# A gated attention and MLP mix on one core: TensorE and VectorE orders fixed by hand, LN1's apply moved to GpSimd, and four smaller moves

## The chip, the cores and the metric

One core of one Trainium2 chip. The metric is device time in microseconds of one execution; a quoted time is the median of the fast runs. "Span" is the length of one profiled execution, about 2 us shorter than its time. The mean granted TensorE clock of each profiled run is given where it matters.

The engines by their names in the profile: PE is TensorE (matmul), DVE is VectorE, ACT is ScalarE, POOL is GpSimd, SP is the sync engine, which here only issues DMA.

## The reference

Input x is 2048 rows of 640 bf16 values; 32 heads of 20.

```python
def _A_ref(x, wqkv, wo):                       # linear attention
    q, k, v = ...                              # x @ wqkv
    pq, pk = phi(q), phi(k)                    # phi(t) = where(t>0, t+1, exp(t)) + 1e-6
    kv  = einsum("bhsd,bhse->bhde", pk, v)
    z   = einsum("bhsd->bhd", pk)
    num = einsum("bhqd,bhde->bhqe", pq, kv)
    den = einsum("bhqd,bhd->bhq", pq, z)[..., None] + 1e-6
    return (num / den) @ wo                    # heads put together again

def _B_ref(x, w1, w2, w3, w4):
    h  = gelu(layernorm(x) @ w1)               # LN1, W1
    hs = concat(four column groups of h, shifted by 1, -1, 2, -2 rows) @ w2
    x1 = x + hs
    return x1 + gelu(layernorm(x1) @ w3) @ w4  # LN2, W3, W4

g = sigmoid((x * gate_w).sum(-1))
return g * A + (1 - g) * B
```

## The kernel before

The 2048 rows are 16 chunks of 128 rows, and 4 tiles of 4 chunks. `pair()` gives one of four PSUM buffers; whatever TensorE writes next needs one that its reader has given back. A framework orders the instructions of each engine and inserts all waits. The stages on TensorE, in order: wk (k for 16 chunks), q, g (x transposed times phi(k)), z, W1 of tile 0, kv, W1 of tile 1, W2 of tile 0, W1 of tile 2, den, W1 of tile 3, then for each tile a W3 and a W4 stage (the first W3 stage also holds the rest of W2, the m products and, before the change, the scaling of phi(q) by 1/den).

The profile's names: pp is a PSUM buffer (PSUM is the memory that TensorE writes to), pk is phi(k), pqT phi(q) transposed, zz the sum z in two bf16 parts, zT its transpose, zbd what den is multiplied with; omg is 1 - g, ehT a transpose on the way to it; r_bf holds ey / den, kvT the masked kv, lnxT a tile of LN1 transposed, hsT the GELU outputs at their shifted places. A "round trip" is VectorE writing a tile, a DMA transposing it, and VectorE reading it again.

Parts:

```python
    def gate_unit():                     # its first part (gate logits, exp into ey) is cut
        ...
        eh = area2.tile([P, 2, TS], BF16, tag="z")
        nc.vector.tensor_copy(eh[:, 0], ey[:])
        nc.vector.tensor_tensor(eh[:, 1], ey[:], eh[:, 0], op=ALU.subtract)
        ehT = area2.tile([P, 2 * CPT, P], BF16, tag="zT")
        nc.sync.dma_start_transpose(ehT[:], eh[:].rearrange("p k s -> p (k s)"))   # round trip 1
        nc.vector.tensor_tensor(omg[:]..., eT[...], eT[...], op=ALU.add)           # omg = 1 - g
        ...
    def z_unit():
        ...                                                                        # matmuls, then
        nc.vector.tensor_copy(zv[:, 0], pt[:, :, 0:HD])
        nc.vector.tensor_tensor(zv[:, 1], pt[:, :, 0:HD], zv[:, 0], op=ALU.subtract)
        nc.sync.dma_start_transpose(zT[:], zz[:])                                  # round trip 2
        nc.vector.tensor_reduce(zc[:], zT[:]..., op=ALU.add)
        ...                                                                        # zbd from zc
    def den_unit():                      # matmuls with zbd and pqT, then
        nc.vector.tensor_scalar_add(pt[:, 0, :], pt[:, 0, :], 1e-6)
        nc.vector.reciprocal(pt[:, 1, :], pt[:, 0, :])
        nc.vector.tensor_tensor(r_bf[:], pt[:, 1, :], ey[:], op=ALU.mult)

    def ln1_tile(t):
        lnxT[t] = lnx_p.tile([P, DC, TS], BF16, name="lnxT")
        for c in range(t * CPT, (t + 1) * CPT):
            ln_stats(mv1[:, c, :], x_sb[:, c, :], st1s[:, c])                      # DVE
        tt = slice(t * CPT, (t + 1) * CPT)
        rsqrt(rstd1[:, tt], mv1[:, tt, 1])                                         # GpSimd
        for c in range(t * CPT, (t + 1) * CPT):
            lnx = work.tile([P, D], BF16, name="ln")                               # 3 buffers
            nc.vector.tensor_scalar(lnx[:], x_sb[:, c, :], mv1[:, c, 0:1], rstd1[:, c:c + 1],
                                    op0=ALU.subtract, op1=ALU.mult)                # "the apply"
            cc = c % CPT
            nc.sync.dma_start_transpose(lnxT[t][:, :, cc * P:(cc + 1) * P], lnx[:])

    def w1_unit(t, fcs):
        ...                                                                        # matmuls on lnxT[t]
            if fc < 4:
                nc.scalar.activation(hsT[:, fc, o:o + TS], pt[:, i, :], ACT.Gelu_apprx_tanh)
            else:                                                                  # the fifth block
                for g in range(4):
                    nc.scalar.activation(hsT[32 * g:32 * (g + 1), 4, o:o + TS],
                                         pt[32 * g:32 * (g + 1), i, :], ACT.Gelu_apprx_tanh)
    ...
    for c in range(NCH):
        k_unit(c)
    for t in range(NT):
        for js in q_split:
            q_unit(t, js)
        if t == 1:
            gate_unit()
    ...
    for fc in range(DC):
        g_unit(fc)
    z_unit()
    ln1_tile(0)
    ln1_tile(1)
    ...                                  # W1 of tile 0, kv, W1 of tile 1, ln1_tile(2), ln1_tile(3)
```

## Time and profile before

| before | value |
|---|---|
| time, median of the first 3 runs | 287.79 us (287.67 to 288.4) |
| profiled span, mean clock | 286.1 us, 0.98 |
| PE busy, POOL busy | 273.3 us, 24.1 us |
| W1 of tile 1 starts | 87.95 us |
| first W3 stage | 114.5 to 143.2 us |

The page of the kernel before, the span in 40 slices of 7.15 us; each digit is tenths of a slice (9 is 90% or more), and PEclk is the granted clock in tenths:

```profile
PE   6999999999967999999899999999999999999994
...
POOL 8500100011213010000001000001000010000000
PEclk9999999999985999999999999999999999999999
```

TensorE is full but for the ends of the span, slices 12 and 13 and a small dip in slice 20, and its clock drops in slices 12 and 13. GpSimd is nearly idle. The waits of TensorE in the kernel before (what it waited for, microseconds in total, times, longest):

```profile
PE pp L285 <- DVE zz L261: 2.3, 1, 2.3
PE pp L358 <- DVE kvT L293: 2.2, 1, 2.2
...
```

Two waits of some weight after the head, one stage: the kv stage (L285) waited for the buffer that VectorE's zz gave back, and W1 of tile 1 (L358) for the one that kvT gave back. The timeline of TensorE in the kernel before (start, length, what, and in brackets the idle time ahead of it):

```profile
75.18 4.49 PE L358 MATMUL pp<-lnxT,w_sb 128*128 128x512 bf16 x20
79.51 1.24 PE L361 MATMUL pp<-lnxT,w1x 128*128 128x512 bf16 x5
83.06 2.65 PE L285 MATMUL pp<-wkq 128*120 128x120 bf16 x30 [2.31 <-DVE zz L261]
87.95 7.33 PE L358 MATMUL pp<-lnxT,w_sb 128*128 128x512 bf16 x20 [2.24 <-DVE kvT L293]
```

The same 20 W1 matmuls took 4.49 us for tile 0 and 7.33 us for tile 1: the clock records show 0.5 from 83.5 to 93.7 us. The Trainium skill says that an idle window takes the array to half its clock and a busy one back ("TensorE: Matmul & The Clock Gate", "What's actually happening"); this trace agrees as to the two states, and shows a drop after only 2.3 us of idle time. So a short wait costs more than its length.

### The profile page before, as it was taken

The numbers are of one execution on the slowest core, as the hardware profiler recorded it, in microseconds if no ns is written. First come the engines' busy times: TensorE is split into PE (matmuls) and PEld (weight loads), VectorE is DVE, ScalarE is ACT, GpSimd is POOL, SyncE is SP. The second block draws the span as 40 slices with busy tenths as digits, with TensorE's granted clock in tenths as the row PEclk, the third lists the DMA queues.
The fourth block names the chain that finished last, engine by engine and source line by source line (L and its number), as shares of the span: only waits on it lengthen the run. The fifth ranks groups of instructions, "written<-read, shape, count | busy, mean of one in ns | idle before, by whom it ended". The sixth has DMA issues, their size and how long they took to land.

```text
span 286.1 us, 4181 instructions
## 1 busy us (share of the span) xinstructions
PE 273.3 (96%) x1730; PEld 162.2 (57%) x1730; DVE 132.6 (46%) x266; ACT 92.0 (32%) x117; POOL 24.1 (8%) x47
## 2 busy tenths in 40 slices
PE   6999999999967999999899999999999999999994
PEld 3677444677542543544377655577655577545772
DVE  1588788888733367485625244034252045100121
ACT  1455435311440529732314022404033304143000
POOL 8500100011213010000001000001000010000000
PEclk9999999999985999999999999999999999999999
DMA  8999884025548804000002400003300007100001
GB/s 207 214 318 363 221 269 136 3 40 98 109 79 231 170 0 92 2 0 0 0 2 66 98 23 0 2 23 69 92 2 0 2 23 112 51 0 0 25 32 37
DMA packets 43464, 22.96 MB, mean 80 GB/s; under 512 B 33670, under 2 KB 42375, under 8 KB 43447
## 3 DMA queue, kind: packets, MB, share of 16 engines
q1 hardware_dynamic: 41669, 19.68, 28.1%
q0 software_dynamic: 464, 2.21, 2.3%
q10 hardware_dynamic: 1314, 0.82, 0.9%
q8 instruction: 13, 0.21, 0.3%
q14 instruction: 4, 0.03, 0.0%
HBM read 11.96 MB, written 2.62 MB: 51 GB/s over the span
## 4 chain that ended last, share of the span: by engine, by line
PE 78%; DVE 8%; DMA 6%; ACT 3%; issue 2%; POOL 1%; DVEq 0%; SPq 0%; ACTq 0%; POOLq 0%
PE pp L450 21%; PE pp L463 21%; PE pp L202 8%; PE pp L460 8%; PE pp L212 7%; PE pp L419 6%; DMA lnxT<-ln 4%; PE pp L358 3%; DMA x_sb<-in_A_x_dram 1%; DMA zT<-zz 1%; DVE st1s L185 1%; DVE ln L347 1%; POOL rstd_191 L182 1%; PE pp L303 1%; ACT ln L437 1%
## 5 line engine op out<-in xcount | busy, mean ns | idle before, releaser
L450 PE MATMUL pp<-lnxT,w_sb 128*128 128x512 bf16 x280 | 63.4, 379 | 1.2 <-ACT h_1268 L452 0.8
L450 PEld LDWEIGHTS <-w_sb 128*128 128x128 bf16 x280 | 27.1, 98 | 32.3 <-issue 2.5
L192 ACT ACTIVATE e<-pp 128x640 bf16<-128x640 f32 (+2 forms) x28 | 21.8, 780 | 24.0 <-PE pp L202 14.8
L460 PE MATMUL pp<-m_sb,pqT 128*128 128x320 bf16 x160 | 27.0, 299 | 0.0
L419 PE MATMUL pp<-w_sb,hsT 128*128 128x320 bf16 x160 | 23.9, 299 | 0.0
L202 PE MATMUL pp<-wkq,xT 128*128 128x320 bf16 x160 | 23.1, 308 | 0.0
L358 PE MATMUL pp<-lnxT,w_sb 128*128 128x512 bf16 x80 | 20.8, 422 | 2.2 <-DVE kvT L293 2.2
L212 PE MATMUL pp<-xT,wkq 128*128 128x512 bf16 x100 | 22.1, 379 | 0.0
L273 PE MATMUL pp<-pk,x_sb 128*128 128x320 bf16 x160 | 21.9, 299 | 0.0
L419 PEld LDWEIGHTS <-hsT 128*128 128x128 bf16 x160 | 15.4, 98 | 8.1 <-issue 0.7
L202 PEld LDWEIGHTS <-xT 128*128 128x128 bf16 x160 | 16.1, 101 | 6.7
L460 PEld LDWEIGHTS <-pqT 128*128 128x128 bf16 x160 | 15.7, 98 | 6.7
L273 PEld LDWEIGHTS <-x_sb 128*128 128x128 bf16 x160 | 15.7, 98 | 6.2
L463 PE MATMUL pp<-w_sb,h_1682 128*128 128x320 bf16 x112 | 16.5, 299 | 0.0
L463 PE MATMUL pp<-w_sb,h_2026 128*128 128x320 bf16 x112 | 16.5, 299 | 0.0
L463 PE MATMUL pp<-w_sb,h_2370 128*128 128x320 bf16 x112 | 16.5, 299 | 0.0
L463 PE MATMUL pp<-w_sb,h_1268 128*128 128x320 bf16 x112 | 16.5, 299 | 0.0
L212 PEld LDWEIGHTS <-wkq 128*128 128x128 bf16 x100 | 9.6, 98 | 11.6 <-issue 0.4
L358 PEld LDWEIGHTS <-w_sb 128*128 128x128 bf16 x80 | 8.3, 107 | 13.8 <-issue 4.5
L326 DVE TENSOR_TENSOR pqT<-pqT,pp 128x1024 bf16<-128x1024 bf16 x10 | 12.1, 1217 | 6.4 <-PE pp L323 6.3
L366 ACT ACTIVATE hsT<-pp 128x512 bf16<-128x512 f32 x16 | 8.6, 596 | 18.8 <-PE pp L358 18.8
L194 DVE SCALAR_TENSOR_TENSOR pk<-pp,e 128x640 bf16<-128x640 f32 x16 | 13.2, 825 | 1.7
(197 smaller groups left out, 280.7 us busy)
## 6 DMA issues: line engine op xcount, KB each, us to landing
out_dram<-oc SPq DMA_DIRECT2D x15, 160.0 KB, 2.0
w_sb<-in_B_w_dram SPq DMA_DIRECT2D x1, 2160.0 KB
w_sb<-in_B_w_dram POOLq DMA_DIRECT2D x1, 2080.0 KB, 11.0
x_sb<-in_A_x_dram SPq DMA_DIRECT2D x3, 640.0 KB, 8.5
wkq<-in_A_wqkv_dram SPq DMA_DIRECT2D x2, 800.0 KB, 9.8
wkq<-in_A_wqkv_dram ACTq DMA_DIRECT2D x2, 400.0 KB, 4.8
w_sb<-in_B_w_dram SPq DMA_DIRECT2D x1, 800.0 KB
wo_sb<-in_A_wo_dram SPq DMA_DIRECT2D x5, 150.0 KB, 9.3
```

What stands on the lines that cost most here:

```text
L192: nc.scalar.activation(ev, src, ACT.Exp)
L194: nc.vector.scalar_tensor_tensor(dst, src, 0.0, ev, op0=ALU.max, op1=ALU.add)
L202: nc.tensor.matmul(pt[:, hf, 0:c1 - c0], lhsT=xT[:, dc, cs], rhs=wk_sb[:, dc, c0:c1], start=(dc == 0), stop=(dc == DC - 1))
L212: nc.tensor.matmul(pt[:, i, :], lhsT=wq_sb[:, dc, j * P:(j + 1) * P], rhs=xT[:, dc, ts_], start=(dc == 0), stop=(dc == DC - 1))
L273: nc.tensor.matmul(pt[:, hf, 0:HD], lhsT=x_sb[:, c, fc * P:(fc + 1) * P], rhs=pk[:, c, hf * HD:(hf + 1) * HD], start=(c == 0), stop=(c == ...
L326: nc.vector.tensor_tensor(sl, sl, pt[:], op=ALU.mult)
L358: nc.tensor.matmul(pt[:, i, :], lhsT=w1_sb[:, dc, CG * fc:CG * fc + P], rhs=lnxT[t][:, dc, :], start=(dc == 0), stop=(dc == DC - 1))
L366: nc.scalar.activation(hsT[:, fc, o:o + TS], pt[:, i, :], ACT.Gelu_apprx_tanh)
L419: nc.tensor.matmul(pt[:, hf, 0:HD], lhsT=hsT[:, fc, 2 + c * P:2 + (c + 1) * P], rhs=w2_sb[:, fc, hf * HD:(hf + 1) * HD], start=(fc == 0), ...
L450: nc.tensor.matmul(pt[:, i, :], lhsT=w3_sb[:, dc, fc * P:(fc + 1) * P], rhs=lnT[:, dc, :], start=(dc == 0), stop=(dc == DC - 1))
L460: nc.tensor.matmul(pt[:, hf, 0:HD], lhsT=pqT[:, j, c * P:(c + 1) * P], rhs=m_sb[:, j, hf * HD:(hf + 1) * HD], start=(j == 0), stop=False)
L463: nc.tensor.matmul(pt[:, hf, 0:HD], lhsT=h2[:, fc, cc * P:(cc + 1) * P], rhs=w4_sb[:, fc, hf * HD:(hf + 1) * HD], start=False, stop=(fc == ...
```

## The change

Its intent: keep the two stalls around kv from arising, by fixing TensorE's and VectorE's orders by hand, by taking LN1's apply off VectorE, by moving the den product ahead of W1 of tile 0, and by moving the scaling out of the crowded first W3 stage into W1. Also a new head (four chunks transposed on TensorE, wk by halves), the fifth block's GELU in one piece with GpSimd copying it to its shifted places, and LN2 chunk by chunk. Cut to its core:

```diff
     def ln1_tile(t):
 ...
-            nc.vector.tensor_scalar(lnx[:], x_sb[:, c, :], mv1[:, c, 0:1], rstd1[:, c:c + 1],
+            nc.gpsimd.tensor_scalar(lnx[:], x_sb[:, c, :], mv1[:, c, 0:1], rstd1[:, c:c + 1],
                                     op0=ALU.subtract, op1=ALU.mult)
 ...
+                hx = hxp.tile([P, TS], BF16, name="hx")
+                nc.scalar.activation(hx[:], pt[:, i, :], ACT.Gelu_apprx_tanh)
                 for g in range(4):
-                    nc.scalar.activation(hsT[32 * g:32 * (g + 1), 4, o:o + TS], pt[32 * g:32 * (g + 1), i, :], ...)
+                    nc.gpsimd.tensor_copy(hsT[32 * g:32 * (g + 1), 4, o:o + TS], hx[32 * g:32 * (g + 1), :])
 ...
+    pe_dve = {mybir.EngineType.PE, mybir.EngineType.DVE}
+    with tc.manual_schedule(engines=pe_dve):
+        ...                                  # head: four chunks transposed on TensorE, wk by halves
+        g_unit(0)
+        ln1_tile(0)
+        g_unit(1)
+        omg_unit()                           # was part of gate_unit, in the q stage
+        z_unit()                             # was after the five g blocks
+        ln1_tile(1)
+        g_unit(2)
+        ln1_tile(2)
+        g_unit(3)
+        ln1_tile(3)
+        g_unit(4)
+        den_unit()                           # was after W1 of tile 2
+        for fcs in w1_split:
+            w1_unit(0, fcs)
+        for gs in ((0, 1), (2, 3), (4, 5)):
+            kv_unit(gs)
+        for i, fcs in enumerate(w1_split):
+            w1_unit(1, fcs)
+            scale_unit(i)                    # the scalings were in the first W3 stage
 ...
+        nb = small.tile([P, 1], F32, name="nb2")            # LN2, for each chunk
+        nc.gpsimd.tensor_scalar(nb[:], mv[:, 0:1], rstd[:], -1.0, op0=ALU.mult, op1=ALU.mult)
 ...
+    with tc.manual_schedule(engines={mybir.EngineType.PE}):
+        ...                                  # W2, W1 of tiles 2 and 3 with 7 scalings, W3 and W4
```

GpSimd, ScalarE and the sync engine keep the orders that the framework finds.

## The prediction

> **What bounds the kernel now.** TensorE: busy 273 of the 286.1 us span (busy shares), 78% of the chain that ended last. From 143 to 282 us its matmuls run back to back (timeline: 0.216 us per 512-column matmul, 0.136 per 320): nothing to win there. What it loses lies earlier:
>
> - Head: warm-up, two transposed chunks, first wk matmul at 6.05 us, nine of them at half clock (0.267 us each) until 8.4 us.
> - The kv stage (80.8 to 96.3 us): 2.3 us idle until VectorE's zz gave back a PSUM pair, kv at half clock (2.65 us), 2.2 us idle until the kvT copies, which sat in VectorE's order behind the 3.5 us zz transpose, then W1 of tile 1 in 8.4 us instead of 5.4. The granted clock is 0.5 from 83.5 to 93.7 us. Together some 8.4 us, the only large loss. The Trainium skill ("TensorE: Matmul & The Clock Gate", "What's actually happening") says an idle window throttles the array; this trace agrees, after only 2.3 us idle.
> - W1 of tile 3 and first W3 stage: 0.5 + 0.5 + 0.8 us of waits for ScalarE.
>
> **What the change does, costed.**
> 1. Head: two more chunks transposed on TensorE (0.53 us each at half clock). The half-wk order hides a DMA wait the trace does not have: the half clock, not wk, made the first unit slow. I expect 0 to 0.6 us lost.
> 2. LN1's apply (16 x 0.36 us) and its waits for the rsqrt leave VectorE. But VectorE's order is now fixed, with two DMA round trips inside: omg and z (3.5 us each). Summed with trace durations from its last phi (55.5): statistics of tile 0 4.2, omg 1.1 + 3.5 + 0.6, zz 1.7, transpose 3.5, zbd 1.3, twelve chunk statistics at 1.04 = 12.5, den 4.8 (the reciprocal 3.36): about 88.5 to 89.5 us.
> 3. TensorE: g, z, den done at 77, W1 tile 0 at 82.3, kv (1.6 at full clock) at 84. Then den's pair and kv's three, all four PSUM pairs, wait for VectorE. W1 tile 1 cannot start before about 89: roughly 5 us idle, then half clock for some 5 us (2 to 3 us lost). The old stall in two pieces returns as one of about the same cost, 7 to 8 us. This is the step that decides.
> 4. Scaling: 10 x 0.32 us of TensorE work stay, only elsewhere. The first W3 stage falls from 28.8 to about 24.3 us, W1 tiles 1 to 3 grow by 3.2. Saved: waits there, about 1.3 us, plus 0.6 in W1 of tile 3, as GELU's four 32-partition pieces (2.4 us ScalarE) become one of 0.6 plus GpSimd copies (estimate 0.6 each from its 0.71 us select of 32x640).
> 5. GpSimd: 16 applies, estimated 0.7 to 1.2 us each from its memset rate (0.9 ns per element); hidden.
>
> Sum: 75.7 + den 1.2 + W1 5.4 + kv 1.6 + stall 5.4 + W1 8.2 + W2 5.4 + W1 10.8 + scaling 3.2 + W3 24.3 + unchanged rest 142.9 = 284.1 us span, time 1.7 more: **285.6 us**, 8 in 10 between 281.5 and 289.5. Faster by over 2%: 0.19; within: 0.77; slower: 0.04.
>
> **What would show it.** Right: TensorE idle near 84 to 89 us, released by VectorE's den or kvT; clock 0.5 after it; no wait at scaling; W3 first stage near 24 us; the rest unchanged. Wrong: no gap over 2 us after kv.
>
> **What would make it wrong.** VectorE reaching den before 84 us removes stall and half clock: about 278 us. The omg or z transpose queued behind LN1's on the DMA queue, or kv's first pair taking den's slot: 287 to 289.

## More of the kernel before

VectorE's group for the apply, and the sync engine's queue, in the kernel before:

```profile
L347 DVE TENSOR_SCALAR ln<-x_sb,mv_190,rstd_191 128x640 bf16<-128x640 bf16 x16 | 6.5, 443 | 5.9 <-POOL rstd_191 L182 4.8 <-DMA lnxT<-ln 1.0
```

```profile
61.26 18.20 SPq L350 DMA_TRANSPOSE lnxT<-ln  x12
82.94 1.33 SPq L262 DMA_TRANSPOSE zT<-zz  x1
```

Sixteen applies are 6.5 us of VectorE in all, 443 ns each (neighbouring records overlap a little). All DMA transposes go through one queue, in one order: z's comes after twelve of LN1's, but those are done by 79.5 us, and it does not wait for them.

## The result, and the profile after

| | before | after |
|---|---|---|
| time, median of 4 runs | 288.1 us (287.67 to 289.18) | 314.55 us (314.14 to 314.86) |
| ratio, 95% interval | 1 | 1.0911 [1.0876, 1.0946] |
| profiled span, clock | 286.1 us, 0.98 | 312.4 us, 0.943 |
| PE busy | 273.3 us | 276.9 us |
| POOL busy | 24.1 us | 85.7 us |

The change is slower by 9.1%, far outside the predicted range. The slices of the kernel after (7.81 us each):

```profile
PE   5999999998480915969999999999999999999995
...
POOL 8301000292089999636120100210102101000000
PEclk9899999999596675899999999999999999999999
```

The hole in TensorE's row is now slices 10 to 18, GpSimd is full in slices 13 to 16, and the clock is low in most of slices 11 to 17. The waits of TensorE, after:

```profile
PE pp L445 <- POOL hsT L377: 10.3, 2, 10.2
PE pp L363 <- DMA lnxT<-ln: 8.6, 1, 8.6
PE pp L323 <- DVE zbd L276: 5.2, 1, 5.2
...
PE pp L363 <- DVE pqT L337: 1.8, 1, 1.8
```

W2 waited 10.2 us for GpSimd's copies, W1 of tile 1 waited 8.6 us for a transposed LN1 tile, den waited 5.2 us for VectorE's zbd. The same stretch of TensorE's timeline, after:

```profile
82.08 2.32 PE L323 MATMUL pp<-pqT,zbd 128*32 128x512 bf16 x20 [5.25 <-DVE zbd L276]
...
90.47 1.76 PE L295 MATMUL pp<-wkq 128*120 128x120 bf16 x30
100.88 0.59 PE L363 MATMUL pp<-lnxT,w_sb 128*128 128x512 bf16 x1 [8.64 <-DMA lnxT<-ln]
...
121.00 7.09 PE L445 MATMUL pp<-w_sb,hsT 128*128 128x320 bf16 x30 [10.15 <-POOL hsT L377]
...
138.86 2.32 PE L363 MATMUL pp<-lnxT,w_sb 128*128 128x512 bf16 x10 [1.81 <-DVE pqT L337]
```

The kv stage itself (L295) now runs at full clock in 1.76 us instead of 2.65, so the half clock of that stage is repaired. What comes before and after it is lost. Thirty W2 matmuls took 7.09 us, where 30 x 0.136 = 4.1 us is full clock. Now who is late? The group of the apply, GpSimd's timeline, and ScalarE's line for the GELU that the copies read, after:

```profile
L352 POOL TENSOR_SCALAR ln<-x_sb,mv_174,rstd_175 128x640 bf16<-128x640 bf16 x16 | 39.9, 2501 | 0.5
```

```profile
62.61 9.97 POOL L352 TENSOR_SCALAR ln<-x_sb,mv_174,rstd_175 128x640 bf16<-128x640 bf16 x4
86.67 0.23 POOL L170 TENSOR_SCALAR rstd_175<-mv_174 128x4 f32<-128x4 f32 x1 [14.09 <-DVE mv_174 L177]
...
88.15 9.96 POOL L352 TENSOR_SCALAR ln<-x_sb,mv_174,rstd_175 128x640 bf16<-128x640 bf16 x4
...
110.95 7.48 POOL L352 TENSOR_SCALAR ln<-x_sb,mv_174,rstd_175 128x640 bf16<-128x640 bf16 x3
118.38 2.56 POOL L377 COPY hsT<-hx 32x512 bf16<-32x512 bf16 x4
```

```profile
90.67 0.60 ACT L374 ACTIVATE hx<-pp 128x512 bf16<-128x512 f32 x1
```

The apply takes 2501 ns on GpSimd; it took 443 ns on VectorE. A tile of four is 10 us. The copies show a second harm: those that W2 of tile 0 needs could have run from 91.3 us, when hx was there, but in GpSimd's order they stand behind the applies of tile 1, of tile 2 and three of tile 3, and came at 118.38 us, though W1 of tile 1 was done at about 110. And between tiles 0 and 1 GpSimd stood idle for 14.09 us, waiting for VectorE's statistics (mv). Why were those late? The sync engine's queue, after:

```profile
65.16 6.17 SPq L355 DMA_TRANSPOSE lnxT<-ln  x3
71.42 2.39 SPq L247 DMA_TRANSPOSE ehT<-eh  x1
73.90 1.25 SPq L355 DMA_TRANSPOSE lnxT<-ln  x1
78.10 1.33 SPq L272 DMA_TRANSPOSE zT<-zz  x1
```

and the one line of VectorE's timeline, after, that waits for it:

```profile
75.85 0.18 DVE L249 TENSOR_TENSOR omg<-ehT 128x16 f32<-128x16 bf16 x1 [14.27 <-DMA ehT<-eh]
```

VectorE had eh ready at 61.6 us. Its transpose stood in the queue behind three LN1 transposes, which came as GpSimd made them, 2.5 us apart. VectorE, whose order is now fixed, waited 14.27 us, and zz, zbd and the statistics of tiles 1 to 3 waited behind it. VectorE's chain (statistics 82.5 to 94.4, den 94.5 to 99.2, kvT to 100.6) and GpSimd's (tile 1 applied at 98.1, its last transpose landed by 100.9) then released W1 of tile 1 at nearly the same time. So at this last step either alone would have kept it until about 100.6 us. They are not two independent causes, though: GpSimd's tile 1 was late because it had waited 14.09 us for VectorE's statistics, and those stood behind VectorE's wait for ehT, which had stood behind GpSimd's tile 0.

The shift, stage by stage, read from the timelines:

| event on TensorE | before | after | shift | grown by |
|---|---|---|---|---|
| wk stage ends | 28.9 | 30.7 | +1.8 | +1.8 |
| g and z end | 75.2 | 76.8 | +1.6 | -0.2 |
| W1 of tile 1 starts | 87.95 | 100.88 | +12.9 | +11.3 |
| W2 of tile 0 starts | 96.2 | 110.1 | +13.9 | +1.0 |
| first W3 stage starts | 114.5 | 145.5 | +31.0 | +17.1 |
| first W3 stage ends | 143.2 | 169.6 | +26.4 | -4.6 |
| end | 286.1 | 312.4 | +26.3 | -0.1 |

Two stretches lose 28 us, the first W3 stage wins 4.6 us (the scalings, 3.2 us, and 1.25 us of waits for ScalarE are gone), and nothing after it moved.

### The profile page after: what moved, and what is told of

It is laid out like the page before. It is cut to its first block, busy times and chain, and to the rows that moved or that the text cites. A ratio compares the mean times of both kernels' runs of the same rounds, so it can differ in the third digit from the quotient of the medians.

```text
span 312.4 us, 4265 instructions
## 1 busy us (share of the span) xinstructions
PE 276.9 (89%) x1726; PEld 163.4 (52%) x1740; DVE 128.0 (41%) x247; ACT 85.1 (27%) x105; POOL 85.7 (27%) x119
## 4 chain that ended last, share of the span: by engine, by line
PE 49%; POOL 15%; DVE 6%; issue 3%; DMA 2%; ACT 2%; SPq 0%; DVEq 0%; POOLq 0%
PE pp L483 19%; PE pp L470 17%; POOL ln L352 10%; PE pp L480 7%; PE pp L445 4%; ACT ln L459 2%; PE pp L363 1%; DMA ehT<-eh 1%; POOL hsT L377 1%; DMA zT<-zz 1%; POOL rstd_175 L171 1%; DVE bnst L175 1%; DVE bnst L176 1%; POOL w_sb L428 0%; SPq L355 0%
## 5 line engine op out<-in xcount | busy, mean ns | idle before, releaser
L352 POOL TENSOR_SCALAR ln<-x_sb,mv_174,rstd_175 128x640 bf16<-128x640 bf16 x16 | 39.9, 2501 | 0.5
L445 PE MATMUL pp<-w_sb,hsT 128*128 128x320 bf16 x160 | 27.1, 323 | 10.3 <-POOL hsT L377 10.3
L445 PEld LDWEIGHTS <-hsT 128*128 128x128 bf16 x160 | 16.5, 105 | 20.7 <-POOL hsT L377 11.0
L202 PE MATMUL pp<-wkq,xT 128*128 128x320 bf16 x160 | 23.8, 310 | 0.0
```

Source lines behind the costliest of these rows:

```text
L202: nc.tensor.matmul(bank[:, 0:HD], lhsT=xT[:, dc, c * P:(c + 1) * P], rhs=wk_sb[:, dc, hf * HD:(hf + 1) * HD], start=(dc == 0), stop=(dc == ...
L352: nc.gpsimd.tensor_scalar(lnx[:], x_sb[:, c, :], mv1[:, c, 0:1], rstd1[:, c:c + 1], op0=ALU.subtract, op1=ALU.mult)
L445: nc.tensor.matmul(pt[:, hf, 0:HD], lhsT=hsT[:, fc, 2 + c * P:2 + (c + 1) * P], rhs=w2_sb[:, fc, hf * HD:(hf + 1) * HD], start=(fc == 0), ...
```

## The experiments

The theory (A): GpSimd's slow apply is the cause, in two ways, its rate (LN1 tiles late, and the copies and LN2's small operations queued behind 40 us of applies) and the sync queue (omg's and z's transposes behind LN1's). The rival (B): the fixed orders, with two round trips inside VectorE's, are the cause, whoever applies; then the move of the scalings, LN2 by chunks, and the head are further suspects. Each run is compared with the kernel before of the same rounds (medians there 287.2 to 287.9 us). Runs of different rounds mostly ran on different chips; where two of them, or one and the change, are set against each other below, remember that the kernels before of these rounds agree only within 0.9 us (288.1 us beside the change). All outputs were correct.

### Who applies LN1, all else as in the change

**e1: ScalarE applies.** The edit:

```diff
-            nc.gpsimd.tensor_scalar(lnx[:], x_sb[:, c, :], mv1[:, c, 0:1], rstd1[:, c:c + 1], ...)
+            nc.scalar.activation(lnx[:], x_sb[:, c, :], ACT.Identity, bias=nb1[:, c:c + 1], scale=rstd1[:, c:c + 1])
```

(nb1 is minus mean times rstd, two small GpSimd operations for each tile.)

> The changed kernel with one part replaced: LN1 is applied on ScalarE (which is idle through most of the g stage) instead of GpSimd; TensorE and VectorE keep their fixed order. Theory A (the slow GpSimd apply, 2.50 us each, is what made the kernel slower: it delays the first LN1 transposes, omg's transpose behind them, and the hsT copies): omg's VectorE wait falls from 14.3 to about 3.5 us, the waits of 5.2, 8.6 and 10.2 us on TensorE go, and only the stall that the prediction named stays (about 5 us, VectorE's den and kvT, then half clock): span about 285, time about 287, 0.91 of the changed kernel. Rival B (the fixed VectorE order with its two DMA round trips is the main cause by itself): the time stays above 300.

Measured: 296.22 us, ratio 1.0302 [1.0235, 1.037]. It lies between the two: 18 of the 26 us came back, and 8 to 9 us over the kernel before stayed. Its waits show a new one: 5.4 us for ScalarE's eviction of g, which the framework had put behind applies in ScalarE's order.

**e2: VectorE applies, as before, but in the fixed order** (one word, `gpsimd` to `vector`).

> The changed kernel with LN1 applied on VectorE as in the kernel before; all else kept. Theory A plus the fixed order: GpSimd is free, so the 10 us wait for the hsT copies goes, but VectorE now waits for each tile's rsqrt and for the work buffers in its fixed order (about 7.4 us a tile instead of 4.2), so den's VectorE part ends near 102 us, W1 of tile 1 starts near 103 and the time is about 300. Rival C (the engine of the apply matters only through GpSimd, the order costs nothing): about 285.

Measured: 310.06 us, ratio 1.0794 [1.0732, 1.0855]. Worse than expected: one wait of 26.5 us for r_bf. In the fixed order VectorE waits at each tile for GpSimd's rsqrt (6.7 us in all) and for a free work buffer (8.4 us), and everything behind waits too. So with VectorE's apply this order costs 22.6 us over the kernel before, without any apply on GpSimd: a point for rival B. Moving the apply off VectorE was right for this order (e1 is 14 us faster); GpSimd was the wrong place.

**e3: GELU of the fifth block in four pieces on ScalarE again**, no GpSimd copies; the apply stays on GpSimd.

```diff
-                hx = hxp.tile([P, TS], BF16, name="hx")
-                nc.scalar.activation(hx[:], pt[:, i, :], ACT.Gelu_apprx_tanh)
                 for g in range(4):
-                    nc.gpsimd.tensor_copy(hsT[32 * g:32 * (g + 1), 4, o:o + TS], hx[32 * g:32 * (g + 1), :])
+                    nc.scalar.activation(hsT[32 * g:32 * (g + 1), 4, o:o + TS], pt[32 * g:32 * (g + 1), i, :], ...)
```

> The changed kernel with GELU's fifth block written straight to hsT by four ScalarE instructions, as before; LN1 stays on GpSimd. Theory A: the 10.2 us wait of W2 for the hsT copies was only a queueing wait behind LN1 applies; it goes, but W1 of tile 3 then waits for its own applies (GpSimd ends them near 121 us), so about 10 to 14 us of 26 come back: time 300 to 305. Rival D (the copies themselves are the expensive part): time below 295.

Measured: 310.75 us, ratio 1.0813 [1.0738, 1.0888]. A miss: the 10.2 us wait went, but only about 4 us came back. The waits of TensorE in this run:

```profile
PE pp L334 <- DVE x L448: 7.8, 1, 7.8
PE pp L363 <- DMA lnxT<-ln: 7.3, 1, 7.3
PE pp L323 <- DVE zbd L276: 5.3, 1, 5.3
```

A wait of 7.8 us took the place of the one removed. Followed back in this trace: the scaling's matmul waits for a PSUM buffer that VectorE's x1 gives back; VectorE stands 10.28 us at the product of x1 and omg, which may overwrite x1 only after ScalarE's LN2 has read it; ScalarE stands 12.83 us for LN2's nb; and nb is a small GpSimd operation behind the applies. So GpSimd's queue is met again three engines on.

**e4: GpSimd's rates**, measured by probes in the kernel before (only the group lines are read; its time means nothing).

```diff
+    for i in range(3):
+        nc.gpsimd.tensor_copy(pa[:], src)
+        nc.gpsimd.tensor_scalar(pa[:], src, mv1[:, 0, 0:1], rstd1[:, 0:1], op0=ALU.subtract, op1=ALU.mult)
+        ...                                  # half the columns; immediates; one operation; f32
+        nc.gpsimd.tensor_tensor(pa[:], src, src, op=ALU.mult)
```

> The kernel before (two x1 buffers fewer, to make room) with extra GpSimd instructions whose results nobody uses, three of each form on 128x640, to measure GpSimd's rate by form: copy bf16, tensor_scalar with two per-partition operands in bf16 (the LN1 apply), the same on 320 elements, with two immediates, with one operation, in f32, and a bf16 tensor_tensor. If the 2.50 us of the apply is GpSimd's own rate for this form, it shows again here at 2.4 to 2.6 us with no bn_stats beside it, and half of it on 320 elements; if it came from sharing SBUF access with VectorE, it falls towards the 0.6 us of a memset of this size.

GpSimd's groups in this run, shapes kept apart (busy us, then mean ns):

```profile
L485 POOL TENSOR_SCALAR pa<-x_sb,mv,rstd 128x640 bf16<-128x640 bf16 x3 | 7.7, 2568 | 0.1
...
L488 POOL TENSOR_SCALAR pa<-x_sb,mv 128x640 bf16<-128x640 bf16 x3 | 5.7, 1886 | 0.2
L486 POOL TENSOR_SCALAR pa<-x_sb,mv,rstd 128x320 bf16<-128x320 bf16 x3 | 4.3, 1436 | 0.1
L491 POOL TENSOR_TENSOR pa<-x_sb 128x640 bf16<-128x640 bf16 x3 | 3.8, 1253 | 0.2
...
L484 POOL COPY pa<-x_sb 128x640 bf16<-128x640 bf16 x3 | 2.2, 719 | 24.8 <-issue 24.7
...
L147 POOL MEMSET emat<- 128x640 bf16 x1 | 0.6, 625 | 0.0
```

and one of the three applies in GpSimd's timeline, with the VectorE instruction that started next:

```profile
92.24 2.51 POOL L485 TENSOR_SCALAR pa<-x_sb,mv,rstd 128x640 bf16<-128x640 bf16 x1
95.79 1.10 DVE L347 TENSOR_SCALAR ln<-x_sb,mv,rstd 128x640 bf16<-128x640 bf16 x2 [8.95 <-POOL rstd L182]
```

The apply's operation takes 2568 ns here too. The apply of the second fence took 2.51 us while VectorE stood idle for 8.95 us, so it is not VectorE's work beside it that makes it slow. It takes 1436 ns for half the columns: (2568 - 1436) / 320 = 3.54 ns for each column. A memset of the same size takes 625 ns, a copy 719, a product of two tiles 1253. The prediction had scaled the apply from the memset; the operation that was really used costs four times that.

### The kernel before with the apply on GpSimd alone

**e12: one word in the kernel before** (`nc.vector.tensor_scalar` to `nc.gpsimd.tensor_scalar` in LN1), all orders left to the framework.

> The kernel before with one word changed: LN1 applied on GpSimd, orders left to the scheduler. GpSimd needs 45 us from 60.7 us on for the four tiles (2.5 us a chunk, 1.3 a tile for rsqrt), so tiles are ready near 73, 85, 96 and 108 us, just about when W1 wants them (75, 83 to 88, 101, 108). If only its rate counts, the time rises little, to 288 to 292. If z's transpose is again queued behind LN1's transposes that wait for GpSimd, VectorE stands and kvT is late: 295 to 310.

Measured: 301.78 us, ratio 1.0513 [1.0473, 1.0553]. One word costs 14.5 us without any fixed order. The sync queue and TensorE in this run:

```profile
63.40 32.81 SPq L350 DMA_TRANSPOSE lnxT<-ln  x12
96.30 1.36 SPq L262 DMA_TRANSPOSE zT<-zz  x1
```

```profile
101.88 7.27 PE L358 MATMUL pp<-lnxT,w_sb 128*128 128x512 bf16 x20 [19.54 <-DVE kvT L293]
```

The same twelve LN1 transposes take 32.8 us instead of 18.2, so z's transpose behind them starts at 96.30 instead of 82.94. VectorE waits 22.8 us for it, kvT comes after that, and TensorE stands for 19.5 us.

**e13 and e14: the z transpose (e14: z's and omg's) issued from ScalarE's queue**, in e12 and in the change.

```diff
-        nc.sync.dma_start_transpose(zT[:], zz[:])
+        nc.scalar.dma_start_transpose(zT[:], zz[:])
```

> The kernel before with LN1 on GpSimd (301.8 us), and z's transpose issued from ScalarE's DMA queue instead of the sync queue, where it stood behind twelve LN1 transposes that wait for GpSimd. The orders of TensorE and VectorE stay the same. If the queue position made the 19.5 us wait for kvT, z's transpose lands about 3.5 us after zz (near 80 us), kvT follows at once, W1 of tile 1 starts near 86 when its LN1 is ready, and the time falls to 287 to 292. If GpSimd's own rate made it, or the transposes of the two queues hold each other off, the time stays at 298 to 303.

> The changed kernel with omg's and z's transposes on ScalarE's DMA queue; orders of TensorE and VectorE the same. If the queue position counts: VectorE's waits of 14.3 us (omg) and 3.4 us (z) become about 3.5 each, tile 1's statistics end near 76 us instead of 86.5, GpSimd works through without its 14 us gap and is done with LN1 near 110 instead of 123.5: time 300 to 304 instead of 314.5. If not: 312 or more.

Measured: 302.44 us, ratio 1.0529 [1.0474, 1.0584], and 314.04 us, ratio 1.0925 [1.0853, 1.0997]. Neither differs from the kernel it was made from; in both, what was expected if the queue position does not count (298 to 303, and 312 or more) is what came. They do not settle the matter, because the edit did not take the wait away: in e13 z's transpose was issued only at 97.8 us, ScalarE stood until then, and TensorE waited 20.5 us for ScalarE's hsT instead; in e14 VectorE's wait for omg's transpose fell from 14.27 to 9.4 us, and its wait for z's rose from 3.39 to 7.0. The Trainium skill ("DMA: Bandwidth & Descriptors", "Latency and other measured facts") says that two DMA transposes of different queues must not be in flight together; that e13's program issues z's only after LN1's of 91.1 to 96.1 us fits that, but the run shows only that a second queue gave no earlier start.

**e16: e12 with the z unit ahead of the five g blocks**, so that z's transpose is in the queue before LN1's. The other orders are the framework's.

```diff
-    for fc in range(DC):
-        g_unit(fc)
-    z_unit()
+    z_unit()
+    for fc in range(DC):
+        g_unit(fc)
```

> The kernel before with LN1 on GpSimd (301.8 us) and the z unit moved ahead of the g blocks, so that z's transpose is issued before any LN1 transpose; GpSimd's and ScalarE's orders do not change. If the queue made the cost: VectorE's 22.8 us wait for z and TensorE's 19.5 us for kvT go, W1 of tile 1 starts near 85 us when its LN1 lands, and the time falls to 287 to 292, so that 10 to 15 of the 14.5 us were the queue's. If GpSimd's rate made the cost: 297 to 302.

Measured: 295.29 us, ratio 1.0262 [1.0191, 1.0333]: between the two expectations. z's transpose was issued at 55.5 us, and VectorE no longer waits for it at all. What is left on TensorE in this run:

```profile
85.98 6.16 PE L358 MATMUL pp<-lnxT,w_sb 128*128 128x512 bf16 x19 [4.21 <-DMA lnxT<-ln]
...
114.53 2.74 PE L358 MATMUL pp<-lnxT,w_sb 128*128 128x512 bf16 x6 [9.00 <-DMA lnxT<-ln]
```

Both waits are for LN1 tiles, of tile 1 and of tile 3, with GpSimd applying from 61.9 us on with hardly a pause. So z first wins back 6.5 of the 14.5 us (301.78 - 295.29). That is not the queue's share, nor are the 7.4 us left (295.29 - 287.89) the rate's: the edit also takes away what the kernel before itself lost around kv (kv starts at 80.00 us here, at full clock, and neither zz nor kvT is waited for), and z first with VectorE's apply was not run. The two waits for LN1 alone are 13.2 us.

### The order, with the apply on ScalarE

In the next four, ScalarE applies LN1, statistics and apply are separate calls, and ScalarE's order too is fixed up to W1 of tile 1.

**e7: the change's VectorE order.**

```diff
+    pe_dve = {mybir.EngineType.PE, mybir.EngineType.DVE, mybir.EngineType.Activation}
         g_unit(0)
         ln1_stats(0)
         g_unit(1)
         ln1_apply(0)
         omg_end(omg_unit())
         z_end(z_unit())
         ln1_stats(1)
         ...                                  # as in the change; applies of tiles 1, 2, 3 later
```

> LN1 applied on ScalarE as in the first experiment, VectorE in the changed kernel's order (omg and z with their round trips inside, all sixteen chunk statistics before den), but ScalarE's order fixed too, so that no eviction stands behind an apply. This is the prediction's own picture without its GpSimd mistake. If the prediction's step 3 was right: TensorE idles 4 to 7 us after kv (or at kv, for a PSUM pair) until VectorE's den at 86 to 90 us, then half clock for some us; span about 285, time 286 to 289. If that stall was imagined: time below 281.

Measured: 290.08 us, ratio 1.0077 [1.0014, 1.014]. Taking GpSimd's apply away and keeping ScalarE's in order gives back 24.5 of the 26.5 us. TensorE in this run:

```profile
85.09 0.71 PE L301 MATMUL pp<-wkq 128*120 128x120 bf16 x10 [2.22 <-ACT hsT L381]
...
88.76 1.04 PE L301 MATMUL pp<-wkq 128*120 128x120 bf16 x10 [1.98 <-DVE r_bf L333]
89.73 0.61 PE L373 MATMUL pp<-lnxT,w_sb 128*128 128x512 bf16 x1
```

W1 of tile 1 starts at 89.73 us. The prediction had said about 89, with a stall behind den and kvT and half clock after it: a stall of that kind is there, once GpSimd is out of the way, with half clock from 87.3 to 94.2 us. It is not quite the one described: the idle time is 4.5 us and lies inside kv, and 2.5 us of it are put down to ScalarE's hsT; the wait that ends last is the one for VectorE's r_bf, done at 88.7 us (predicted: 88.5 to 89.5). The time is just above the 286 to 289 us expected.

**e6: a better order.** z ahead of the g blocks, both transposes started before their results are needed, den after the third g block.

```diff
+        zT = z_unit()
         g_unit(0)
         ln1_stats(0)
         g_unit(1)
         ln1_apply(0)
+        z_end(zT)
+        ehT = omg_unit()                     # start of the round trip
         ln1_stats(1)
         g_unit(2)
         ln1_apply(1)
+        omg_end(ehT)                         # its end
+        den_unit()
         g_unit(3)
         ...
```

> As the run with ScalarE's apply and fixed order, with the order on VectorE changed so that nothing waits for a round trip: z first, its end after tile 0's statistics, omg's end after tile 1's, den after the third g block and before the statistics of tiles 2 and 3. If the order is what costs: VectorE is through with den by about 74 us, no TensorE gap over 1 us from 52 us to the first W3 stage except about 2 us at the scaling units, no half clock: span about 277, time about 279, 3% under the kernel before. If PSUM or ScalarE binds instead, gaps of several us stay at W1.

Measured: 286.81 us, ratio 0.997 [0.992, 1.002]. A miss by 8 us: the stall around kv went, but in W1 2.2 us of waits for ScalarE's GELU and the 1.8 us wait for a scaled pqT (there in e7 too) stayed, and half clock from 108.5 to 115.3 us with them.

**e8: e6 with the product of x1 and omg put off to the W4 stage** (`tensor_scalar_mul` moved from `w2_unit` to `w4_unit`), because the 1.8 us wait was VectorE standing at that product for ScalarE's LN2, with the scaling of pqT behind it.

> The last one with the multiplication of x1 by omg put off to the W4 stage, so that VectorE does not wait for ScalarE's LN2 between two scaling steps. If the 1.8 us wait of W1 tile 3 for a scaled pqT (seen in the changed kernel and the first two experiments) comes from that, it goes and the time falls by 1.5 to 2.5 us against the last one; else equal within 0.5 us.

Measured: 285.82 us, ratio 0.9935 [0.9882, 0.9989]. The 1.8 us wait is gone, but the time is only 1 us under e6 (1.5 to 2.5 were expected), with runs that overlap: the waits for ScalarE's GELU grew from 2.2 to 3.5 us.

**e10: ScalarE's order fixed through W1 of tiles 2 and 3 and the first W3 stages as well**, with LN2's applies at chosen places, LN1's statistics and the applies of tiles 2 and 3 earlier, and den after the last g block.

```diff
-        ln = work.tile([P, D], BF16, name="ln")      # in w2_unit
-        nc.scalar.activation(ln[:], x1[:], ACT.Identity, bias=nb[:], scale=rstd[:])
+    def ln2_apply(t, cc): ...
 ...
             w1_unit(2 + i // 3, w1_split[i % 3])
             scale_unit(3 + i)
+            if i < CPT:
+                ln2_apply(0, i)
```

> A version meant to beat both: LN1 on ScalarE, VectorE's new order with all statistics in the g stage and den at its end, tile 2's apply before W1 of tile 0, x1 times omg in the W4 stage, and ScalarE's order fixed in the W1 stage of tiles 2 and 3 so that no GELU stands behind an LN2 apply. If the remaining gaps of the last version (0.8, 0.5, 0.4 and 2.7 us on ScalarE and a transpose, then half clock, 1.7 us) are what is left, span 277 to 279, time 278 to 281, 2.5 to 3.5% under the kernel before. If something else binds (PSUM, VectorE at W2), it stays at 284 to 286.

Measured: 281.28 us, ratio 0.979 [0.9754, 0.9826], span 279.2 us at a clock of 1.0: at the upper edge of what was expected, 2.1% under the kernel before. The waits of TensorE over 0.5 us after the head that remain:

```profile
PE pp L376 <- ACT hsT L381: 1.2, 1, 1.2
PE pp L301 <- ACT hsT L381: 0.6, 1, 0.6
```

**e11: e8 with the apply back on GpSimd**, and **e17: that with the GELU in four pieces on ScalarE**, so that no copies stand behind the applies. They ask whether a good order saves the move to GpSimd.

```diff
-            nc.scalar.activation(lnx[:], x_sb[:, c, :], ACT.Identity, bias=nb1[:, c:c + 1], scale=rstd1[:, c:c + 1])
+            nc.gpsimd.tensor_scalar(lnx[:], x_sb[:, c, :], mv1[:, c, 0:1], rstd1[:, c:c + 1],
+                                    op0=ALU.subtract, op1=ALU.mult)
```

> The kernel with the new order and the late multiplication (285.8 us), LN1 put back on GpSimd. If GpSimd's 16 applies of 2.5 us are a cost by themselves, whatever the order: its last apply ends near 106 us, W1 and W2 wait for it, time 294 to 302. If a good order hides them (they are 40 us of an engine that is else idle): 288 or less, and the order alone was at fault.

> The new order with LN1 on GpSimd (301.0 us) and GELU's fifth block written by four ScalarE instructions, so that W2 waits for no GpSimd copy. If the 13.1 us wait for the copies was all that GpSimd's rate cost there: 286 to 289, as with LN1 on ScalarE. If W1 of tile 3 and LN2's rsqrt then wait for GpSimd's last applies (near 108 us): 292 to 298.

Measured: 300.99 us, ratio 1.0482 [1.0443, 1.0522], with one wait of 13.1 us for the hsT copies; and 298.18 us, ratio 1.036 [1.0309, 1.0412]. The order does not save it: e11 is 15 us over e8. In e17 the copies are gone and 12 us of the 15 stay (298.18 - 285.82). ScalarE's timeline in e17 shows what took the copies' place:

```profile
112.81 0.92 ACT L473 ACTIVATE ln<-x,nb,rstd 128x640 bf16<-128x640 f32 x1 [10.96 <-POOL nb L471]
```

ScalarE waited 10.96 us for nb, a one-column operation of LN2 on GpSimd that stood behind the last applies of LN1. VectorE then waited 8.29 us for ScalarE, and TensorE 5.9 us for VectorE, the chain of e3 again. From 62.5 to 110.2 us GpSimd does little but rsqrt and applies in this run (a DMA issue of 1.4 us, a gap of 0.26). Whatever GpSimd does next for the critical path is late by that much.

**e5: omg back in the q stage**, else as the change (A: it frees VectorE of the 14.27 us wait).

```diff
         g_unit(1)
-        omg_unit()
 ...
                 gate_unit()
+                omg_unit()
```

> The changed kernel with omg's steps put back into the q stage, right after the gate; LN1 stays on GpSimd. It takes omg's transpose out of the place behind three LN1 transposes that wait for GpSimd. Theory A2 (queueing behind GpSimd doubles its cost): VectorE's 14.3 us wait goes, den waits for zbd 0 to 2 us instead of 5.2, the applies of tile 1 start about 72 us instead of 88 and GpSimd works without its 14 us gap, so tile 3's last apply ends near 107 instead of 123: time 300 to 305. Rival: if the queue order did not matter, it stays within 2 us of the changed kernel's 314.5.

Measured: 313.44 us, ratio 1.0897 [1.0845, 1.0949]. A miss: the wait for ehT is gone, but now z's transpose stands behind four LN1 transposes instead, VectorE waits 12.2 us for it, and TensorE waits 10.4 us for LN1 and 12.1 us for the copies. Taking one round trip out of the queue hands its wait to the next.

### The head

**e9: the changed head alone, in the kernel before** (loads, four transposes, wk by halves; 5 rounds).

```diff
+        for hf in range(2):
+            for c0 in (0, 2):
+                pt = pair()
+                for i in range(2):
+                    k_half(pt[:, i, :], c0 + i, hf)
+                    if hf == 0 and c0 == 0:
+                        xT_unit(2 + i)
```

> The kernel before with the changed head alone: x chunks 2 and 3 transposed on TensorE, first four chunks by halves of wk, fixed TensorE and VectorE order to the end of the wk stage. The prediction said 0 to 0.6 us lost, because the first unit was slow from the half clock and not from wk. Expected: the wk stage ends 0 to 1.7 us later than in the kernel before (the changed kernel and six experiments show 29.1 to 30.75 us against 29.0, depending on where the half clock falls), time +0 to +0.6%; if the halves hide a real wait, it is faster by 0.3% or more.

Measured: 289.3 us, ratio 1.006 [1.0018, 1.0103]: a loss at the upper end of what was expected for this run. In microseconds it is about 1.7 (0.6%), three times the 0 to 0.6 us that the prediction gave the head. The wk stage ends at 30.3 instead of 28.9 us.

**e15: e10 with the head of the kernel before** (5 rounds).

> The best version (281.3 us) with the head of the kernel before (two chunks transposed on TensorE, whole k units). The head alone cost 0.6% on the kernel before; if that adds up, 279 to 280.5 us, 2.5 to 2.9% under the kernel before; if the half clock at the start moves instead, within 0.3% of 281.3.

Measured: 279.47 us, ratio 0.9723 [0.9685, 0.9761]; span 278.1 us at a clock of 1.0. It is the fastest here, 2.8% under the kernel before and 11% under the change (279.47 / 314.55 = 0.888, from different rounds).

## Why the prediction was wrong

**The step that failed is the fifth.** It read: "GpSimd: 16 applies, estimated 0.7 to 1.2 us each from its memset rate (0.9 ns per element); hidden." Measured: 2.50 us each, 39.9 us in all (after), and not hidden. The memset rate itself was right (625 ns for 640 columns in e4, 0.98 ns each); the error was to carry it over to a two-operation `tensor_scalar`, which costs four times as much. "Hidden" then failed with it: four applies are 10 us for each tile, and GpSimd's order also holds rsqrt, the hsT copies and LN2's small operations, all needed by engines that TensorE waits for.

**How that became 28 us.** The prediction's own sum beside the trace:

| term | predicted | measured |
|---|---|---|
| g and z end | 75.7 | 76.8 |
| den, W1 of tile 0, kv and the stall, to W1 of tile 1 | 13.6 (to 89.3) | 24.1 (to 100.9) |
| W1 of tile 1, W2, W1 of tiles 2 and 3, scaling | 27.6 | 44.6 |
| first W3 stage | 24.3 | 24.1 |
| the rest | 142.9 | 142.8 |
| span | 284.1 | 312.4 |

- The second row missed by 10.5 us. On VectorE's path the error is one number: the omg round trip was given 3.5 us and took 14.27, 10.8 us more. The prediction named this danger ("The omg or z transpose queued behind LN1's on the DMA queue") and gave it 287 to 289 us: right in kind, and far too small, because an LN1 transpose was thought to come about every 1 us and came every 2.5. GpSimd's path ended at the same time (tile 1 landed by 100.9 us), but only because it had waited for VectorE behind that same round trip.
- The third row missed by 17 us: 10.15 of waiting for the copies, about 3.2 of W2 at half clock (36 matmuls in 7.09 + 0.99 us, 4.9 at full clock), and 3.1 of smaller waits. The prediction had no queue behind the applies.
- "No wait at scaling" failed too, by 1.8 us: W1 of tile 3 waits for pqT, which VectorE scales only after it has waited for ScalarE's LN2. e8 takes this wait away by moving one product.
- The head, given 0 to 0.6 us, costs about 1.7 us alone (e9).

**What held.** The first W3 stage falls to 24.1 us. The rest is unchanged. And the third step, which "decides", described a real stall: e7, which has the change's VectorE order and ScalarE's apply, starts W1 of tile 1 at 89.7 us. It was small beside what the fifth step hid. The fifth step is not the whole error, though: e7's 290.08 us still lies above the predicted 281.5 to 289.5, and the head's real cost and the wait for pqT (1.81 us, and ten W1 matmuls in 3.90 us after it instead of 2.33) were not in its sum.

**Shown, and how much.** GpSimd's apply is the main cause: alone in the kernel before it costs 14.5 us (e12), in the better order 15 us (e11 against e8), and taking it out of the change gives back 18 us (e1) or, with ScalarE's order fixed as well, 24.5 us (e7). In e12 both the shared queue (22.8 us of VectorE waiting behind it) and the rate (in e16, with z out of the queue's way, 13.2 us of waits for LN1) are seen at work. The rival, that the orders are the cause, holds for a part: with VectorE's apply the change's order costs 22.6 us (e2), and with ScalarE's it is still 3.3 us slower than the better one (e7 against e6). e10 is another 4.5 us under e8, but it fixes more of ScalarE's order and moves den, statistics and applies as well, so this is not ScalarE's order alone.

**Open.** How the change's own 26 us divide between queue and rate: e5 and e14 tried to take the queue's part out of it and did not, since the waits for the transposes moved or shrank by too little. For the framework's order it is open too: e16 lacks its control, z first with VectorE's apply. In e1 against e7, the fixed ScalarE order and the later applies came together and were not told apart. LN2 by chunks was never undone alone.

## What to carry to other kernels

Before moving work to an idle engine, measure that very operation there, at its shape, and do not scale it from another operation; then follow everything that shares the engine's order and the DMA queue behind it, because idle time is not slack once other engines wait for what comes next. When an engine's order is fixed by hand, start each DMA round trip well ahead of its use and put other work between the two, for an in-order engine passes every late transfer on to all that follows. Orders fixed by hand were worth having in the end, but not this change's order: it took another one, LN1 on ScalarE, ScalarE's order fixed as well and the old head to reach 279.5 us against 287.2.

## What the Trainium skill lacked or had wrong

- "GPSIMD Engine Reference", "4.1 Engine selection", says of elementwise work that GpSimd is about 2x slower than VectorE for two-input operations and that one-input is "roughly line-rate". The apply has one tile as input and took 2.50 us on GpSimd and 0.44 us on VectorE here, 5.6 times as long; it was even slower than GpSimd's product of two tiles (1.25 us). The page's advice to use VectorE for elementwise work holds; its factor misleads for `tensor_scalar`.
- The same page, "3.1 Elementwise — side-by-side cycle accounting", gives 1.03 cycles for each element for a loop body of up to two operations; at the 1.2 GHz of its "1. Specifications" that is an estimate of 0.86 ns. `tensor_scalar` with two operations took 3.54 ns for each column (e4), and one operation instead of two saved 0.68 us of 2.57. Beside `tensor_tensor`, no page has rates by operation: memset 0.63, copy 0.72, `tensor_tensor` 1.25, `tensor_scalar` 1.89 (one operation) and 2.57 us (two), for 128 x 640 bf16.
- "TensorE: Matmul & The Clock Gate", "What's actually happening", ties the drop to a whole idle window of 3.4 us. The kernel before fell to half clock at 83.5 us after 2.3 us of idle time and a sparse kv stage. That less than a whole window can be enough is not said in that section; further down, the page does tell of a kernel whose clock fell through frequent short idles, without a length for them.
- "DMA: Bandwidth & Descriptors", "Latency and other measured facts", says to serialize transposes of different queues. It does not say what that means for a schedule: a second queue gave the urgent transpose no earlier start (e13: issued at 97.8 us, against 96.3 on the one queue), and put ScalarE to waiting as well.
